# Top-k attention and capacity-limited MoE: the weights of a pair of units, all mask products first, then all second score products

## Chip, cores and metric

The kernel runs on one core of one Trainium2 chip. The metric is the device time of one execution in microseconds (us). Engines are named as in the profile: PE is the matrix engine, PEld its loads of stationary operands, DVE the vector engine, ACT the scalar engine, POOL the GpSimd engine.

## The reference, cut to what matters

```python
scores = (q @ k.T) / 8                      # 8 batches x 8 heads, 576 x 576, D = 64
kth    = 32nd largest of each row
scores = where(scores >= kth, scores, -1e9)
attn   = exp(scores - max); attn = attn / (sum + 1e-9)
x      = attn @ v                           # -> 4608 tokens x 512
...
# then a top-1 MoE: 8 experts, each keeps the 80 tokens of the highest gate weight,
# out[tok] = gate * (relu(x[tok] @ w1[e]) @ w2[e]), all other rows are 0
```

The change lies in the attention alone: in the step that turns a row's 32nd-largest score into the weights `exp(score)` of the scores that are kept.

## The kernel before

The attention treats two heads of a batch at a time, 32 such head pairs (`NP`) in all. A head pair has q, k and v of both heads side by side: `qT` and `kT` are 128 partitions by 576 columns, head 0 on partitions 0 to 63 and head 1 on 64 to 127. The 576 rows of a head are cut in four tiles of 128 and a tail of 64 (`t` = 0 to 4). A *unit* is one head's tile of 128 rows; the tails of both heads together are one unit. So a head pair has nine units, and a *pair of units* is the same tile of both heads.

For each unit:

- `front` (L190, L195): score products for the pair with rows on the partitions, into PSUM `sp` (one buffer), copied by ACT to `s`. These are the scores that are searched.
- `parts`, `search` (L202 to L227): DVE finds the 32nd-largest value, by maxima of six slices, three rounds of eight, and a last count that needs ACT (L218) and POOL (L219).
- `drop` (L249): DVE writes a bf16 `mask`, which is the row's maximum for scores that are kept and that plus one for scores that are dropped.

For each pair of units:

- `turn_w` (L265 to L273): the scores once more, now turned, with keys on the partitions, into PSUM `ab` (one buffer; a bank for each head, four chunks of 128 keys) and `cc` (the last 64 keys of both heads, two buffers, shared with the small logits tile `lp`). Two matmuls add up in each place. The mask product (L265) has the bf16 mask as stationary operand and a diagonal of large negative numbers (`minus`) as moving one, so it turns the mask and pushes dropped scores far below zero. The second score product (L269) has `kT` as stationary operand, in float32, 64 rows of the array for each head. ACT then takes the exponential (L272 for `ab`, L273 for `cc`) into `wT`.
- `back` (L287, L289): the weights times v, and their sum, into another part of `cc`.

`front` and `turn_w` both use matmuls over 64 rows of the array (one head each); the mask product uses all 128 rows; the products for the last 64 keys and those of `back` have 64 output columns.

The order is written out by hand. `run` goes through steps i = 0, 1, 2 ...; each engine gets its instructions in the order of the steps and works them off strictly in that order. In step i DVE starts unit i and advances the searches of units i-1, i-2 and i-3; PE gets, in this order, `turn_w` for the pair that unit i-3 completes, `front` for the pair that unit i+2 begins (or, where there is none, the turning of a next head pair's q and k), `back` for the pair that unit i-4 completes, and, once in a head pair, the turning of the normalised output `xn` and its logits `lp` (`norm`). Nine steps are one head pair; this is called a *round* below. The part that matters inside `turn_w`:

```python
for c in range(NK):                # 5 chunks of keys
    for h in range(2): mask product (h, c)     start=True
    for h in range(2): score product (h, c)    stop=True
```

After the attention `judge` and `finish` choose the tokens and do the experts. A second, slower attention (`batch`) stands in a branch for inputs where the search fails.

Of the kernel before, what the change touches and what calls it, by code (L numbers as in the profile page):

```python
# [24 lines left out]
def kernel(  # L25
# [11 lines left out]
    nc = tc.nc  # L37
    B, H, S, D = q.shape
# [8 lines left out]
    P = 128  # L47
    HP = H // 2
    NP = B * HP
    NF = S // P  # L50
    TL = S - NF * P
    NK = NF + 1
# [60 lines left out]
    class Attention:  # L113
# [137 lines left out]
        def turn_w(self, n, t):  # L251

            qT, kT = self.turned[n]
            i = n * UPP + 2 * t
            m = P if t < NF else TL
            masks = [self.mask.pop(i), self.mask.pop(i + 1)] if t < NF else [self.mask.pop(i)] * 2
            eye = [minus, minus] if t < NF else [minus[:, :TL], minus[:, TL:]]
            ab = self.ps_w.tile([P, 2, NF, P], F32, name="ab", tag="ab")
            cc = self.ps_c.tile([P, 512], F32, name="cc", tag="cc")
            rows = slice(t * P, t * P + m)  # L260
            for c in range(NK):
                ks = slice(c * P, min(c * P + P, S))
                for h in range(2):
                    d = slice(D * h, D * h + D)
                    nc.tensor.matmul(ab[:, h, c, :m] if c < NF else cc[d, :m], lhsT=masks[h][:, ks], rhs=eye[h],  # L265
                                     start=True, stop=False)
                for h in range(2):
                    d = slice(D * h, D * h + D)
                    nc.tensor.matmul(ab[:, h, c, :m] if c < NF else cc[d, :m], lhsT=kT[d, ks], rhs=qT[d, rows],  # L269
                                     start=False, stop=True)  # L270
            wT = self.rows.tile([P, 2 * NF + 1, P], F32, name="wT", tag="wT")
            nc.scalar.activation(wT[:, : 2 * NF, :m], ab.rearrange("p h c r -> p (h c) r")[:, :, :m], Act.Exp, scale=scale)  # L272
            nc.scalar.activation(wT[:, 2 * NF, :m], cc[:, :m], Act.Exp, scale=scale)  # L273
            self.w[n, t] = wT, cc
# [430 lines left out]
```

## Time and profile before

The time is 1617.32 us, the median of 3 runs (1616.72 to 1620.83). The profiled execution has a span of 1610.5 us at a mean granted clock of 0.826.

| What | Value |
|---|---|
| start and first loads | the first 23 us |
| attention | 23 to about 1432 us |
| choosing of tokens, experts | about 1432 to 1610 us |
| mask products, L265 | 1600 matmuls, the last at 1432.1 us |
| second score products, L269 | 3200 matmul records (two passes for each float32 product) |
| one exponential of `ab`, L272, at 128 rows | 1.02 us |
| one copy of scores to `s`, L195, of two full units | 1.13 us |

A float32 product appears as two matmul records, one for each pass. Matmuls overlap in the engine and their ends are modelled, so costs are read from the distance between starts. The granted clock is a share of full speed: 1.00 or 0.50 in any short stretch, and 0.83 on average over the attention.

### The profile page before, as it was taken

What the parts mean: (1) busy time and instruction counts of PE and PEld (TensorE: products, weight loads), DVE (VectorE), ACT (ScalarE), POOL (GpSimd) and SP (SyncE); (2) the same over time, 40 slices, a digit from 0 to 9 for tenths busy, and PEclk for the clock granted to TensorE, in tenths of its full rate; (3) what the DMA queues carried; (4) which work ended last, traced back from release to release, by engine and by line L of the source; (5) the groups of instructions that cost most, each with busy time, mean ns of one, the idle gap of its engine ahead of it and who ended that gap; (6) DMA issues with size and microseconds to landing.
All of it is one profiled execution on the core that took longest, in us unless ns stands there. A gap on an engine that the chain in (4) does not pass through costs nothing.

```text
span 1610.5 us, 38356 instructions
## 1 busy us (share of the span) xinstructions
PE 1311.5 (81%) x14862; PEld 936.5 (58%) x14862; DVE 1124.7 (70%) x5095; ACT 682.4 (42%) x1374; POOL 513.0 (32%) x501
## 2 busy tenths in 40 slices
PE   6889888888888888888888888888888888861787
PEld 4556555555555665555555556655555556550687
DVE  5777777777777777786777777777877777838211
ACT  3454444444444544444444445444444444420010
POOL 2333333333333333333333332333333333320111
PEclk9888788887888887888878888878888788775699
DMA  4022222222111122222221111111111110021270
GB/s 119 9 76 83 83 69 57 57 57 57 38 43 42 49 57 56 57 57 57 57 57 32 46 29 26 31 31 31 31 31 31 31 31 9 9 73 39 74 289 25
DMA packets 154591, 85.94 MB, mean 53 GB/s; under 512 B 118304, under 2 KB 136736, under 8 KB 154400
## 3 DMA queue, kind: packets, MB, share of 16 engines
q1 hardware_dynamic: 153376, 80.78, 17.6%
q0 software_dynamic: 1024, 2.62, 0.5%
q8 instruction: 118, 1.93, 0.5%
q14 instruction: 73, 0.60, 0.1%
HBM read 63.19 MB, written 20.19 MB: 52 GB/s over the span
## 4 chain that ended last, share of the span: by engine, by line
PE 70%; DVE 17%; ACT 11%; issue 2%; POOL 0%; DMA 0%; POOLq 0%; DVEq 0%; ACTq 0%
PE ab L269 19%; PE sp L190 15%; PE ab L265 9%; PE cc L287 9%; ACT s L195 5%; DVE mask L249 4%; DVE cand L202 4%; PE cc L269 4%; DVE pick L227 3%; PE sp L165 3%; PE lp L322 2%; PE yp L613 2%; ACT wT L272 2%; DVE cand L222 2%; PE cc L265 2%
## 5 line engine op out<-in xcount | busy, mean ns | idle before, releaser
L219 POOL TENSOR_TENSOR y<-s,y 128x576 f32<-128x576 f32 x288 | 416.7, 1447 | 891.9 <-ACT y L218 888.1
L202 DVE MAX8 cand<-s 128x8 f32<-128x96 f32 x1728 | 428.7, 248 | 253.2 <-ACT s L195 253.1
L269 PE MATMUL ab<-qT,kT 64*128 64x128 f32 (+1 forms) x2560 | 359.2, 363 | 0.0
L272 ACT ACTIVATE wT<-ab 128x1024 f32<-128x1024 f32 (+1 forms) x160 | 150.2, 939 | 415.8 <-PE ab L269 413.7
L265 PE MATMUL ab<-minus,mask 128*128 128x128 bf16 (+1 forms) x1280 | 197.8, 233 | 150.7 <-DVE mask L249 132.2
L190 PE MATMUL sp<-kT,qT 64*128 64x288 f32 (+1 forms) x1280 | 275.3, 565 | 48.3 <-ACT s L195 25.7
L224 DVE MAX8 w<-y 128x8 f32<-128x576 f32 x288 | 214.6, 745 | 92.9 <-POOL y L219 92.9
L269 PEld LDWEIGHTS ab<-qT,kT 64*128 64x128 f32 x2560 | 228.1, 218 | 68.5 <-issue 18.5
L249 DVE TENSOR_SCALAR mask<-s,thr,top 128x576 bf16<-128x576 f32 x288 | 264.9, 920 | 0.3
L265 PEld LDWEIGHTS <-mask 128*128 128x128 bf16 (+1 forms) x1600 | 103.8, 104 | 255.7 <-DVE mask L249 145.7
L287 PEld LDWEIGHTS cc<-vb,wT 128*64 128x64 f32 x4608 | 210.5, 163 | 67.2 <-issue 52.7
L195 ACT ACTIVATE s<-sp 128x1152 f32<-128x1152 f32 (+1 forms) x160 | 165.7, 1035 | 181.0 <-PE sp L190 180.8
L287 PE MATMUL cc<-vb,wT 128*64 128x65 f32 x4608 | 241.6, 251 | 0.0
L218 ACT ACTIVATE y<-s,w 128x576 f32<-128x576 f32 x288 | 222.8, 774 | 18.7 <-DVE w L213 18.6
L190 PEld LDWEIGHTS sp<-kT,qT 64*128 64x128 f32 (+1 forms) x1280 | 140.6, 233 | 128.9 <-ACT s L195 55.8
L227 DVE SCALAR_TENSOR_TENSOR pick<-past,cnt,w 128x9 f32<-128x9 f32 x288 | 140.4, 487 | 0.2
L222 DVE MATCH_REPLACE8 cand<-top,cand 128x48 f32<-128x48 f32 x576 | 110.2, 191 | 0.0
L213 DVE MAX8 top<-cand 128x8 f32<-128x48 f32 x576 | 110.0, 191 | 0.1
L287 PE MATMUL cc<-vr,wT 128*64 128x65 f32 x1152 | 101.8, 245 | 0.0
L269 PE MATMUL cc<-qT,kT 64*64 64x128 f32 (+1 forms) x640 | 79.7, 335 | 0.0
L289 ACT COPY xu<-cc 128x130 f32<-128x130 f32 (+1 forms) x160 | 42.3, 265 | 80.2 <-PE cc L287 80.1
L287 PEld LDWEIGHTS cc<-vr,wT 128*64 128x64 f32 x1152 | 74.8, 161 | 0.0
(165 smaller groups left out, 991.3 us busy)
## 6 DMA issues: line engine op xcount, KB each, us to landing
w<-in_moe_w_dram SPq DMA_DIRECT2D x32, 512.0 KB, 4.5
w<-in_moe_w_dram SPq DMA_DIRECT2D x8, 2048.0 KB, 11.9
out_dram<-zero SPq DMA_DIRECT2D x9, 1024.0 KB, 8.3
qn<-in_q_dram SPq DMA_DIRECT2D x64, 128.0 KB, 2.7
kn<-in_k_dram SPq DMA_DIRECT2D x64, 128.0 KB, 2.7
vb<-in_v_dram SPq DMA_DIRECT2D x64, 128.0 KB, 2.4
xd<-xn SPq DMA_DIRECT2D x32, 256.0 KB, 2.4
qn<-in_q_dram SPq DMA_DIRECT2D x32, 32.0 KB, 2.5
```

Source lines behind the costliest of these rows:

```text
L190: nc.tensor.matmul(o, lhsT=qT[d, t * P : t * P + m], rhs=kT[d, j * HS : (j + 1) * HS], start=True, stop=True)
L195: nc.scalar.activation(s[:, : g * S].rearrange("p (j c) -> p j c", c=HS), ps[:, : 2 * g, :HS], Act.Copy, scale=TINY)
L202: nc.vector.max(out=cand[:, j, :], in_=s[:, j * S // NG : (j + 1) * S // NG])
L218: nc.scalar.activation(y, s, Act.Sign, bias=w9[:, 7:8], scale=-1.0, accum_out=cnt)
L219: nc.gpsimd.tensor_tensor(out=y, in0=s, in1=y, op=Alu.mult)
L224: nc.vector.max(out=w9[:, 8:], in_=y)
L227: nc.vector.scalar_tensor_tensor(out=pick, in0=past, scalar=cnt, in1=w9[:, 7:], accum_out=self.thr[:, i : i + 1], op0=Alu.is_equal, op1=Al ...
L249: nc.vector.tensor_scalar(self.mask[i], s, self.thr[:, i : i + 1], top[:, 0, 0:1], op0=Alu.is_lt, op1=Alu.add)
L265: nc.tensor.matmul(ab[:, h, c, :m] if c < NF else cc[d, :m], lhsT=masks[h][:, ks], rhs=eye[h], start=True, stop=False)
L269: nc.tensor.matmul(ab[:, h, c, :m] if c < NF else cc[d, :m], lhsT=kT[d, ks], rhs=qT[d, rows], start=False, stop=True)
L272: nc.scalar.activation(wT[:, : 2 * NF, :m], ab.rearrange("p h c r -> p (h c) r")[:, :, :m], Act.Exp, scale=scale)
L287: nc.tensor.matmul(cc[r : r + TL, o], lhsT=wT[:, h * NF + c if c < NF else 2 * NF, r : r + TL], rhs=vb[:, c, h, :] if c < NF else vr[:, h, ...
```

## The change

In `turn_w` the loop over chunks that holds both kinds of product becomes two loops. The first does all mask products, head by head (for each head its five chunks); the second does all score products, chunk by chunk, the two heads in turn. The matmuls, their operands and their number are the same, and so is everything outside this loop. Since a bank of `ab` now has four open sums at once, `start=True` is kept only for the first product in each bank (chunk 0) and for the last chunk, which has its own bank. The purpose is that products of one kind follow each other in the array.

```diff
+            keys = [slice(c * P, min(c * P + P, S)) for c in range(NK)]
+            heads = [slice(D * h, D * h + D) for h in range(2)]
+            dst = [[ab[:, h, c, :m] for c in range(NF)] + [cc[heads[h], :m]] for h in range(2)]
+
+            for h in range(2):
+                for c in range(NK):
+                    nc.tensor.matmul(dst[h][c], lhsT=masks[h][:, keys[c]], rhs=eye[h], start=c in (0, NF), stop=False,
+                                     skip_group_check=True)
             for c in range(NK):
-                ks = slice(c * P, min(c * P + P, S))
                 for h in range(2):
-                    d = slice(D * h, D * h + D)
-                    nc.tensor.matmul(ab[:, h, c, :m] if c < NF else cc[d, :m], lhsT=masks[h][:, ks], rhs=eye[h],
-                                     start=True, stop=False)
-                for h in range(2):
-                    d = slice(D * h, D * h + D)
-                    nc.tensor.matmul(ab[:, h, c, :m] if c < NF else cc[d, :m], lhsT=kT[d, ks], rhs=qT[d, rows],
-                                     start=False, stop=True)
+                    nc.tensor.matmul(dst[h][c], lhsT=kT[heads[h], keys[c]], rhs=qT[heads[h], rows], start=False, stop=True,
+                                     skip_group_check=True)
```

## The prediction, made before the changed kernel was run

> **What bounds the kernel now.** I read the page first: busy times, then the chain that ended last (shares of the span by engine, then by line).
>
> ```profile
> PE 1311.5 (81%) x14862; PEld 936.5 (58%) x14862; DVE 1124.7 (70%) x5095; ACT 682.4 (42%) x1374; POOL 513.0 (32%) x501
> ...
> PE 70%; DVE 17%; ACT 11%; issue 2%; POOL 0%; DMA 0%; POOLq 0%; DVEq 0%; ACTq 0%
> PE ab L269 19%; PE sp L190 15%; PE ab L265 9%; PE cc L287 9%; ACT s L195 5%; DVE mask L249 4%; DVE cand L202 4%; PE cc L269 4%; DVE pick L227 3%; PE sp L165 3%; PE lp L322 2%; PE yp L613 2%; ACT wT L272 2%; DVE cand L222 2%; PE cc L265 2%
> ```
>
> PE carries 70% of the chain, and the lines of the change (L265, L269, into ab and cc) hold 34% of the span, some 548 us, or 3.4 us for each of the 160 calls of turn_w. So the change acts on the path. Next, the waits from 300 to 1400 us (total, times, longest):
>
> ```profile
> DVE cand L202 <- ACT s L195: 188.1, 71, 3.9
> PE ab L265 <- DVE mask L249: 95.9, 38, 3.9
> PE ab L265 <- ACT wT L272: 14.5, 25, 0.6
> ```
>
> PE waits for DVE's mask once in a round, DVE about three times for fresh scores: a loop. PE's timeline shows it (start, us, what, idle before):
>
> ```profile
> 647.37 1.24 PE L190 MATMUL sp<-kT,qT 64*128 64x288 f32 x8
> ...
> 649.86 0.23 PE L265 MATMUL ab<-minus,mask 128*128 128x128 bf16 x1
> 653.95 0.29 PE L265 MATMUL ab<-minus,mask 128*128 128x128 bf16 x1 [3.85 <-DVE mask L249]
> 654.16 0.80 PE L269 MATMUL ab<-qT,kT 64*128 64x128 f32 x4
> ```
>
> A front ends at 648.64, ACT copies it by 649.80, DVE needs 4.1 us for its step up to the mask (653.89), and only then turn_w goes on, with the next front behind it. One mask product (head 0) had run before the wait; head 1's held all the rest. Such waits end at 565.09, 609.04 and 653.95; over 28 rounds a round lasts 44.36 us.
>
> Last, the loads of stationary operands, around a chunk of turn_w and around the change from lp to masks:
>
> ```profile
> 620.48 0.11 PEld L265 LDWEIGHTS <-mask 128*128 128x128 bf16 x2
> 620.70 0.30 PEld L269 LDWEIGHTS ab<-qT,kT 64*128 64x128 f32 x4
> 621.12 0.11 PEld L265 LDWEIGHTS <-mask 128*128 128x128 bf16 x2
> ```
>
> ```profile
> 628.32 0.53 PEld L322 LDWEIGHTS lp<-wg,xT 128*128 128x128 f32 x4
> 628.68 0.21 PEld L265 LDWEIGHTS <-mask 128*128 128x128 bf16 x2
> 628.99 0.30 PEld L269 LDWEIGHTS ab<-qT,kT 64*128 64x128 f32 x4
> ```
>
> In the chunk PEld stands idle for 104 ns before the score loads and for 121 ns before the next mask loads. From lp to mask, both on all 128 rows and columns, the load starts (628.684) while the lp matmul that began at 628.682 runs. A change of the array's shape empties it; a change of type alone does not.
>
> **What the Trainium skill says.** TensorEngine Tiling (Array Packing), Key Properties: changing the tiling mode drains the engine. The trace agrees, with the two idle times above. TensorE: Matmul & The Clock Gate, Part 2, says that loads are pulled ahead of running matmuls; the lp case agrees. The same page, Part 1, has a free-running window of 3.41 us, after an idle one of which the clock is halved. The trace agrees on the window (below), though a stretch with 2.83 us of PE busy was also followed by half clock. PSUM — Partial Sum Buffer, The four PSUM rules: the start flag clears the marks of a whole bank, which is why the change keeps one start for each bank; this costs no time and no run here shows it.
>
> **The change, part by part.** Nothing is added or taken away; order and flags change. All starts are from the trace.
>
> A full-clock chunk before, 640 ns: the two masks start 66 ns apart (620.482, 620.548), 147 ns later the score loads start, and 422 ns later the next chunk's mask loads (two passes 213 ns apart, then the emptying). Four chunks 2.56 us, the last mask pair 0.175, the last score pair 0.365: 3.10 us.
>
> After, at full clock: four masks of a head need 66 + 55 + 55 ns (55 is the distance of the pair at 628.794, whose loads were ahead), then 147 to empty: 0.33 us. That head's fifth mask has 64 output columns, another shape: 0.18 us. For two heads 1.01 us. Scores: 422 ns for the first chunk and for three more chunks two passes each at about 107 (transposes of the same size, L165, start 109 apart): 1.06 us. Last pair 0.365. Sum 2.44 us, so 0.66 us less. Shape changes fall from nine to five.
>
> At half clock (chunks at 609.626 and 610.681: 1.06 us): before 4 x 1.06 + 0.25 + 0.48 = 4.97; after 2 x (0.54 + 0.25) + (0.73 + 6 x 0.213) + 0.48 = 4.07 us; 0.90 less. The pace of 107 was not seen for this product. Its ends are 107, and about 160 if each pass still waits for part of its load; then a block saves only 0.34 at full clock.
>
> A second gain: the order by head puts all of head 0's masks (0.50 us) before the first one of head 1. In the block that waits for head 1's mask they lie in the wait. Nothing is queued behind them that could have run.
>
> Now a round, in us from the end of the long wait (609.04 = 0), before and then after. Block t=1 runs 0 to 4.70, mostly at half clock; after, head 1's masks 0.5, scores 2.0, last pair 0.48: ends at 3.0. The tail front 4.70 to 6.65 follows, ACT has it at 7.33, DVE waits for it and makes the next mask at 10.28: all 1.7 earlier. Block t=2 starts 11.44, after 9.75, and ends 14.6, after 12.5. Then 5.3 us of xn, front, back and lp, unchanged. Block t=3 starts 19.9, after 17.8; its ab is done at 22.39, after 19.94 (2.14 into the block), and the exponential holds up the tail block until 23.49, after 21.04; DVE's mask for it, at 22.69 and after 20.99, is ready just in time. The tail block takes 3.47 us, partly at half clock; it has 64 moving columns, and I take 0.6 off, between 0.42 (full) and 0.93 (half). The front after it ends at 29.2, after 26.1. Back and turning of q and k are unchanged; block t=0 starts 35.3, after 32.2, and takes 2.44 for 3.10. Its front ends 39.6, after 35.85; scores at 40.8 and 37.0. DVE could begin that step at 39.2 before and 36.1 after, so the scores still end the wait. Plus 4.07 of DVE: 44.9 before, 41.1 after. The round loses 3.75 us of the 4.3 or so that PE saves. DVE's own work, 34.5 us busy and 2.5 of waits for POOL in a round, is no bound yet.
>
> **The clock.** Cut in windows of 3.41 us, the round shows (us, then busy of PE, PEld, DVE, ACT, POOL, then granted clock):
>
> ```profile
> 606.17:609.58 3.41, 0.54 (x5) 0.40 (x5) 3.41 (x7) 0.87 (x2) 3.26 (x3) 1.00 0.00 0
> 609.58:612.99 3.41, 3.41 (x23) 2.05 (x20) 3.32 (x19) 0.07 (x1) 0.66 (x2) 0.50 0.46 123
> ...
> 630.06:633.47 3.41, 2.83 (x32) 1.99 (x30) 3.41 (x13) 1.95 (x4) 1.35 (x1) 1.00 0.02 5
> 633.47:636.89 3.42, 3.42 (x26) 2.57 (x26) 3.07 (x10) 0.77 (x2) 1.40 (x1) 0.50 0.01 2
> ```
>
> The long wait brings half clock on, and so does the stretch around the wait for the exponential. 44.36 us is 13.0 windows: rounds seem tied to the windows. Twelve windows are 40.96, 3.41 less. Between 3.41 and 3.75 I take 3.6; 31 rounds (36 to 1406 us) give 111 us, and 1617 - 111 = 1506.
>
> **Rivals.**
>
> - *Favoured, 0.60*: as worked out, 1506.
> - *Smaller gain from grouping, 0.14*: passes at 160 ns, or drains that stay. Some 2.2 us a round: 1617 - 68 = 1549. For it: no run of such products without a shape change is in the trace. Against it: L165 at 109, and the front's loads, which run ahead.
> - *The clock gains too, 0.12*: the long wait falls from 3.85 to about 3.4 us and may no longer fill a window. Block t=1 then takes 1.9, its front 1.2: 1.8 us more a round, 5.4 x 31 = 167, so 1450. Against it: DVE's 37 us come close, and a full window idle wasn't needed for the other slowdown.
> - *The clock takes back most, 0.09*: the wait for the exponential grows from 0.58 to about 0.8 us, and another two windows a round fall to half clock: a block 1.63 and a front 1.0 more, 2.6 us. Gain 1.0 a round: 1586.
> - *Slower, 0.05*: two such stretches a round, 5.2 against 3.6: 31 x 1.6 = 50, so 1667. Only the sensitivity of the clock speaks for it.
>
> **How the numbers follow.** The prediction is the favoured case. The range goes from just under the third case to just under the fourth, 1445 to 1580; outside lie the slower case, most of the fourth and a margin of the third. Slower by over 0.3% is 0.05; within 0.3% is 0.03, from the upper edge of the fourth; faster 0.92.
>
> **What would show it.** Right: masks in fours about 55 ns apart; score passes 107 to 110 apart with no PEld idle between chunks; a full-clock block of 2.4 us; rounds of about 41 us; PE's wait for masks still once a round at about 3.4; DVE's waits for s smaller by 1.5 us or more a round. Wrong: passes at 160; a round of 43 or more with a lower granted clock than 0.83; new waits of PE for masks at blocks t=2 or the tail, which would mean that DVE has become the bound.

## The result, and the profile after

The changed kernel takes 1421.72 us, the median of 4 runs (1420.56 to 1422.79), against 1617.15 us before: a ratio of 0.879, with a 95% interval of 0.877 to 0.880. That is 195 us less, where 111 were predicted, and the time lies below the stated range of 1445 to 1580.

The first lines of the page of after are the busy times, then the clock granted in 40 slices, then the chain that ended last:

```profile
PE 1125.7 (79%) x14862; PEld 863.7 (61%) x14862; DVE 1130.2 (80%) x5095; ACT 678.0 (48%) x1374; POOL 506.5 (36%) x501
...
PEclk9999899989899998998998999889989989855899
...
PE 68%; DVE 14%; ACT 14%; issue 3%; POOL 1%; DMA 0%; POOLq 0%; DVEq 0%; ACTq 0%
PE sp L190 17%; PE ab L271 14%; PE cc L289 12%; PE ab L267 6%; ACT s L195 5%; DVE mask L249 4%; PE cc L267 3%; ACT wT L274 3%; PE cc L271 3%; PE lp L324 3%; PE yp L615 3%; DVE cand L202 3%; DVE pick L227 2%; ACT y L218 2%; PE sp L165 2%
```

The same matmuls keep PE busy for 186 us less. The lines of the change, now L267 and L271, fell from 34% of the span to 26%, and PE still leads the chain. The mean granted clock rose from 0.826 to 0.874, which the favoured case of the prediction had not counted on.

All of the gain is in the attention: from the last turned score product to the end it is 178.1 us before and 177.4 after. A round, over 24 rounds of the trace, fell from 44.38 to 38.67 us.

The waits of DVE and PE from 300 to 1200 us (total, times, longest):

```profile
DVE cand L202 <- ACT s L195: 90.3, 67, 2.3
PE ab L267 <- DVE mask L249: 80.8, 23, 3.5
PE ab L267 <- ACT wT L275: 20.3, 23, 0.9
```

They are the same three as before. DVE's waits for scores fell from 7.6 to 3.8 us a round. PE still waits once a round for a mask, 3.5 us instead of 3.9, and for the exponential 0.88 us instead of 0.58.

PE's timeline around the wait, then PEld's in an undisturbed block (start, us, what, idle before):

```profile
566.26 0.40 PE L267 MATMUL ab<-minus,mask 128*128 128x128 bf16 x4
566.59 0.24 PE L267 MATMUL cc<-minus,mask 128*64 128x128 bf16 x1
570.34 0.42 PE L267 MATMUL ab<-minus,mask 128*128 128x128 bf16 x4 [3.51 <-DVE mask L249]
```

```profile
578.09 0.94 PEld L267 LDWEIGHTS <-mask 128*128 128x128 bf16 x10
579.09 0.97 PEld L271 LDWEIGHTS ab<-qT,kT 64*128 64x128 f32 x16
580.18 0.20 PEld L271 LDWEIGHTS cc<-qT,kT 64*64 64x64 f32 x4
```

Head 0's five mask products now run ahead of the wait, as predicted. The sixteen loads of the score products go through in 0.97 us without a gap. By the single starts, masks follow each other at 66, 56 and 56 ns, score passes at 105 to 112 ns (the two heads side by side, 6 or 7 ns apart), and each change of shape among the masks costs 147 to 172 ns from the last start to the next load. From its first to its last matmul start a block at full clock takes 2.26 us, where it took 2.90 before (medians of blocks t=0).

What the prediction missed shows in windows of 3.41 us (us, then busy of PE, PEld, DVE, ACT, POOL, then granted clock), around the long wait and around the tail block:

```profile
567.18:570.59 3.41, 0.25 (x4) 0.23 (x4) 3.41 (x9) 0.87 (x2) 3.26 (x3) 1.00 0.00 0
570.59:574.00 3.41, 3.41 (x28) 2.72 (x27) 3.41 (x18) 0.93 (x2) 0.94 (x2) 0.50 0.36 99
574.00:577.42 3.42, 2.67 (x38) 1.58 (x36) 2.04 (x13) 2.20 (x6) 1.04 (x1) 1.00 0.72 164
587.66:591.07 3.41, 2.53 (x40) 1.92 (x36) 3.41 (x17) 1.94 (x4) 1.81 (x2) 1.00 0.00 0
591.07:594.49 3.42, 3.42 (x30) 2.27 (x30) 1.97 (x9) 1.60 (x3) 0.31 (x1) 0.50 0.00 0
594.49:597.90 3.41, 2.54 (x40) 1.93 (x37) 2.31 (x15) 1.83 (x6) 1.43 (x1) 1.00 0.00 0
```

Half clock still comes on at the same two places in a round, but it mostly ends after one window; in 8 of 24 rounds the first stretch still lasts three. Before, it lasted two or three windows at the first place and two at the second. Counted over 24 rounds, half clock fell from 15.1 to 9.1 us a round.

### The profile page after: what moved, and what is told of

The parts are those of the page before. It is cut to its first block, busy times and chain, and to the rows that moved or that the text cites. A ratio compares the mean times of both kernels' runs of the same rounds, so it can differ in the third digit from the quotient of the medians.

```text
span 1420.7 us, 38356 instructions
## 1 busy us (share of the span) xinstructions
PE 1125.7 (79%) x14862; PEld 863.7 (61%) x14862; DVE 1130.2 (80%) x5095; ACT 678.0 (48%) x1374; POOL 506.5 (36%) x501
## 4 chain that ended last, share of the span: by engine, by line
PE 68%; DVE 14%; ACT 14%; issue 3%; POOL 1%; DMA 0%; POOLq 0%; DVEq 0%; ACTq 0%
PE sp L190 17%; PE ab L271 14%; PE cc L289 12%; PE ab L267 6%; ACT s L195 5%; DVE mask L249 4%; PE cc L267 3%; ACT wT L274 3%; PE cc L271 3%; PE lp L324 3%; PE yp L615 3%; DVE cand L202 3%; DVE pick L227 2%; ACT y L218 2%; PE sp L165 2%
## 5 line engine op out<-in xcount | busy, mean ns | idle before, releaser
L219 POOL TENSOR_TENSOR y<-s,y 128x576 f32<-128x576 f32 x288 | 408.6, 1419 | 704.2 <-ACT y L218 702.4
L274 ACT ACTIVATE wT<-ab 128x1024 f32<-128x1024 f32 (+1 forms) x160 | 150.1, 938 | 297.8 <-PE ab L271 296.3
L190 PE MATMUL sp<-kT,qT 64*128 64x288 f32 (+1 forms) x1280 | 251.9, 523 | 48.4 <-ACT s L195 25.8
L267 PE MATMUL ab<-minus,mask 128*128 128x128 bf16 (+1 forms) x1280 | 124.8, 222 | 143.5 <-DVE mask L249 116.2
L289 PEld LDWEIGHTS cc<-vb,wT 128*64 128x64 f32 x4608 | 194.3, 152 | 65.3 <-issue 50.8
L218 ACT ACTIVATE y<-s,w 128x576 f32<-128x576 f32 x288 | 222.8, 774 | 20.1 <-DVE w L213 19.8
L267 PEld LDWEIGHTS <-mask 128*128 128x128 bf16 (+1 forms) x1600 | 109.0, 103 | 202.3 <-DVE mask L249 154.9
L249 DVE TENSOR_SCALAR mask<-s,thr,top 128x576 bf16<-128x576 f32 x288 | 231.7, 805 | 0.3
L289 PE MATMUL cc<-vb,wT 128*64 128x65 f32 x4608 | 222.7, 239 | 0.0
L271 PE MATMUL ab<-qT,kT 64*128 64x128 f32 (+1 forms) x2560 | 215.3, 315 | 0.0
L271 PEld LDWEIGHTS ab<-qT,kT 64*128 64x128 f32 x2560 | 182.5, 216 | 11.5
L227 DVE SCALAR_TENSOR_TENSOR pick<-past,cnt,w 128x9 f32<-128x9 f32 x288 | 185.4, 644 | 0.2
L267 PE MATMUL cc<-minus,mask 128*64 128x128 bf16 (+1 forms) x320 | 78.4, 245 | 0.0
L271 PE MATMUL cc<-qT,kT 64*64 64x128 f32 (+1 forms) x640 | 77.2, 325 | 0.0
```

The lines of the kernel that those rows point to most:

```text
L190: nc.tensor.matmul(o, lhsT=qT[d, t * P : t * P + m], rhs=kT[d, j * HS : (j + 1) * HS], start=True, stop=True)
L218: nc.scalar.activation(y, s, Act.Sign, bias=w9[:, 7:8], scale=-1.0, accum_out=cnt)
L219: nc.gpsimd.tensor_tensor(out=y, in0=s, in1=y, op=Alu.mult)
L227: nc.vector.scalar_tensor_tensor(out=pick, in0=past, scalar=cnt, in1=w9[:, 7:], accum_out=self.thr[:, i : i + 1], op0=Alu.is_equal, op1=Al ...
L249: nc.vector.tensor_scalar(self.mask[i], s, self.thr[:, i : i + 1], top[:, 0, 0:1], op0=Alu.is_lt, op1=Alu.add)
L267: nc.tensor.matmul(dst[h][c], lhsT=masks[h][:, keys[c]], rhs=eye[h], start=c in (0, NF), stop=False, skip_group_check=True)
```

## The experiments

Two theories stood for the shorter stretches. **Streaming**: half clock ends after a window in which PE streams enough columns; the old block, which emptied the array twice a chunk, streamed too few. **Round length**: a shorter round merely meets the windows elsewhere. In the diffs, `mask(h, c)` and `score(h, c)` stand for the two matmuls of `turn_w`, and `old()` and `new()` for the two orders of the change. The first four runs shared runs of the kernel before (1616.92 us), the next four others (1615.87), the last one others (1616.85).

### One block of the five in the new order, and the other four

```diff
-            new()
+            new() if t == 1 else old()      # only_t1
+            new() if t != 1 else old()      # but_t1
```

> New order in block t=1 alone (the one behind the long wait), old order in the other four. Theory 'streaming': half clock ends after a window in which PE streams enough columns; the old block at half clock streams too few because of its emptyings, the new one enough. It expects the first half-clock stretch of a round to shrink from 6.8 or 10.2 us to 3.4, the second to stay at 6.8, half clock per round 15 to about 11 us, and the time near 1546 us (1.45 us a round from the block itself and about 0.9 from the clock). Theory 'round length': the stretches shrank because a shorter round meets the windows of the clock elsewhere. It expects both stretches as before and 1617 - 31 x 1.45 = 1572 us.

> The complement: old order in block t=1, new order in the other four. 'Streaming' expects the first stretch to stay at 6.8 us or more and the second to shrink to 3.4, and, with 0.64 us from three blocks and 1.1 from the tail block, about 1617 - 31 x 3.0 = 1524 us or a little less. 'Round length' expects both stretches to shrink, since the round is nearly as short as with the whole change: 1450 to 1470 us.

Measured: 1516.55 us for the new order in block t=1 alone (ratio 0.938, 0.937 to 0.940), 1463.41 us for the complement (0.904, 0.902 to 0.907). In 24 rounds, the first stretch of half clock and the second lasted so many windows:

| Kernel | first stretch | second stretch | half clock, us a round |
|---|---|---|---|
| before | 2 (14 times), 3 (10) | 2 (24) | 15.1 |
| only_t1 | 1 (16), 2 (7), 3 (1) | 2 (15), none (9) | 9.0 |
| but_t1 | 2 (17), 3 (4), 4 (3) | 1 (13), none (11) | 10.1 |
| after | 1 (16), 3 (8) | 1 (24) | 9.1 |

The first stretch shortened where block t=1 was in the new order, and never fell under two windows where it was not. The second stretch of only_t1 kept its two windows in 15 rounds, with the old order at that place; in the other 9 it did not come at all, so where a block falls among the windows matters too. Round length alone doesn't explain the table: but_t1 has a round of 39.9 us, near that of after (38.7), and its first stretch stayed long. Here are the first two windows of a first stretch in only_t1, then in but_t1, and the second and third of the stretch of the kernel before whose first one, at 609.58, the prediction shows:

```profile
568.78:572.19 3.41, 3.31 (x27) 2.77 (x29) 3.41 (x20) 0.40 (x1) 1.29 (x2) 0.50 0.30 90
572.19:575.60 3.41, 2.65 (x30) 1.45 (x28) 2.10 (x13) 2.44 (x6) 0.76 (x1) 1.00 0.73 166
```

```profile
590.57:593.99 3.42, 3.42 (x22) 2.10 (x21) 3.42 (x19) 0.00 (x0) 0.85 (x2) 0.50 0.39 110
593.99:597.40 3.41, 3.02 (x18) 1.32 (x14) 0.09 (x1) 1.54 (x3) 0.00 (x0) 0.50 0.68 153
```

```profile
612.99:616.41 3.42, 2.67 (x14) 1.19 (x12) 0.02 (x1) 1.82 (x4) 0.00 (x0) 0.50 0.69 156
616.41:619.82 3.41, 3.41 (x30) 2.37 (x32) 3.41 (x16) 1.77 (x3) 1.40 (x1) 0.50 0.69 171
```

PE counts as busy throughout the first window of but_t1, with 22 matmuls, and half clock goes on; in only_t1 the new order has 27 in 3.31 us, and full clock follows. So PE's busy time, as the profile models it, doesn't show what the clock follows.

A count of moving columns does. Take each matmul's moving columns, times the share of the 128 rows that it uses, and twice for a float32 pass: such passes start 107 ns apart where bf16 products of 128 columns start 55 apart. Split a matmul at a window's edge by that pace, which is half as fast at half clock. In the kernel before, from 200 us on to 190 us before the end (357 windows), every window that half clock followed then has at most 3072, and every one that full clock followed at least 3174, whichever clock it ran at itself. In all eleven traces a limit of 3140 puts 3269 of 3287 windows right; the best limit on PE's busy time fails in 342, the best on the number of matmuls in 288. The window at 568.78 of only_t1 has 3242; that at 590.57 of but_t1 has 2532, and its second 3100 (one of the 18 that fail). In the kernel before, 609.58 has 2560, 612.99 has 2816 and 616.41 has 5003; the one at 630.06 of the prediction, busy for 2.83 us and followed by half clock, has 3072. The count was fitted to these traces, and no run here tests it on another kernel. It is what 'streaming' asks for: PE is busy throughout at 609.58 before and at 570.59 in after, both at half clock, and the old block moves 2560 columns in that time, the new one 3360.

'Streaming' had expected 1546 and 1524 us, 30 and 60 more than was measured. 'Round length' was 55 us too high for only_t1, but the 1463 of but_t1 lie in its 1450 to 1470. So the times don't decide between the two; the first stretches do. A part that neither had is in the table: in 9 and 11 of 24 rounds the second stretch does not come at all. The two gains, 100 and 153 us, sum to more than the 195 of the whole change, so they overlap.

### The order among the masks

```diff
-            for h in range(2):                 # the change: five changes of shape
-                for c in range(5): mask(h, c)
+            for h in range(2):                 # four_four: three
+                for c in range(4): mask(h, c)
+            for h in range(2): mask(h, 4)
+            for c in range(5):                 # by_chunk: three, heads in turn
+                for h in range(2): mask(h, c)
```

> New order, but the mask products as four of head 0, four of head 1, then both of the last 64 keys: three changes of shape within a block in place of five. If emptying sets the price of a change of shape, a full-clock block falls from 2.26 us (first to last start) to about 1.98; four such blocks a round give up to 1.1 us a round: 1388 to 1403 us. If DVE has become the bound, 1415 to 1425.

> New order, but the mask products chunk by chunk with the heads in turn: the same three changes of shape as four_four, but only one mask product can run ahead of the wait for head 1's mask. Blocks without the wait as in four_four. Block t=1 has about 0.2 us (full clock) to 0.4 (half clock) more behind the wait: 6 to 12 us slower than four_four. If running head 0's masks in the wait is worth nothing, the same as four_four.

Measured: 1390.58 us (0.860, 0.858 to 0.861) and 1393.99 us (0.862, 0.860 to 0.863). Two changes of shape fewer take a full-clock block from 2.26 to 1.985 us, as expected to the hundredth, and the kernel another 31 us below the change; in that, half clock fell as well, from 9.1 to 8.0 us a round. By the blocks, a change of shape among the mask products costs 0.14 us at full clock.

Running head 0's masks inside the wait is worth 3 us or nothing; the intervals touch. In by_chunk block t=1, where nearly all of it ran at half clock, does take up to 3.39 us, against 3.07 in four_four, but its rounds sit at 37.5 to 37.7 us, eleven windows, with each stretch one window long in all 24 rounds. In four_four eight of 24 first stretches last three windows, and half clock is 8.0 us a round against 6.8. So what by_chunk loses in the block it gets back from the clock.

### The last score products first, where the next front has the other shape

```diff
-            for c in range(5):
+            for c in ((4, 0, 1, 2, 3) if t in (0, 4) else range(5)):
                 for h in range(2): score(h, c)         # otherwise as four_four
```

> four_four, but in blocks t=0 and tail the score products of the last 64 keys come first, so that the block ends in the shape in which the next front begins. An emptying less, twice a round, 0.1 to 0.15 us each, against an exponential that starts some 0.36 us later behind the front: 1380 to 1391 us.

Measured: 1389.62 us (0.859, 0.857 to 0.862), against 1390.58 for four_four: no difference that can be told. A round takes 37.62 us, against 37.55 in four_four, so what an emptying less may have given was taken back; fifteen of 24 first stretches of half clock now last three windows, and half clock is 9.1 us a round against 8.0.

### Matmuls that nothing reads in PE's waits

These kernels keep all their work and add matmuls whose result lies in unused columns of `cc`, so that PE isn't idle while it waits.

```diff
+            if t == 4:
+                for _ in range(16): matmul(cc[:, 258:386], lhsT=minus, rhs=minus)
+            if t == 1:                          # 34 in before_fill, 30 in the others;
+                for _ in range(34):             # inside the masks in four_fill and edges_fill
+                    matmul(cc[:, 258:512], lhsT=minus, rhs=masks[0][:, :254])
```

before_fill, after_fill, four_fill and edges_fill have the order of before, after, four_four and edges. four_fill has the second filler alone, the others have both.

> The old order, with matmuls that nothing reads in the two waits: 34 of 254 columns (about 3.6 us) ahead of block t=1, 16 of 128 (about 0.9 us) ahead of the tail block. 'Streaming' expects both half-clock stretches to go: half clock per round from 15 us to near 0, and, with the block, front and tail at full clock, some 4 us a round: about 1493 us. That would be the clock's part of the old time. If the clock follows from something else than PE's idling, 1617 or, with fillers too long, more.

> four_four with 30 such matmuls of 254 columns in block t=1, between head 0's masks and head 1's. 'Streaming' expects the first stretch to go and the second to stay: half clock from 7.7 to about 3 us a round, 1 to 2 us a round off: 1330 to 1360 us. If DVE is the bound by now, 1380 to 1390.

> edges with both fillers (30 of 254 columns inside block t=1, 16 of 128 ahead of the tail block). 'Streaming' expects almost no half clock in a round and DVE (33.6 us busy and about 1 of waits) as the next bound: a round of 35 us, 1310 to 1330 us. If the clock isn't set by PE's idling, 1385 or more.

> The changed order with both fillers, 30 of 254 columns ahead of block t=1 and 16 of 128 ahead of the tail block, so that it stands beside before_fill with the clock nearly full in both. If the change is worth on its own account what the blocks show at full clock (0.64 us from each of three, some 0.5 from the tail block, 0.64 plus 0.5 from the one with the wait: 3.6 us a round), the round goes from 38.97 to about 35.4, near DVE's floor of some 34: about 1338 us, and the rest of the 195 us (1617 to 1422), some 80, is the clock's. If the clock's part is small, nearer 1260 to 1290; if the change mostly helps the clock, 1400 or more.

| Kernel | us | ratio to before | round, us | half clock, us a round |
|---|---|---|---|---|
| before | 1617 | 1 | 44.38 | 15.1 |
| before_fill | 1449.66 | 0.897 (0.894 to 0.899) | 38.96 | 0.85 |
| after | 1421.72 | 0.879 (0.877 to 0.880) | 38.67 | 9.1 |
| after_fill | 1306.35 | 0.808 (0.806 to 0.809) | 34.72 | 0 |
| four_fill | 1297.32 | 0.802 (0.801 to 0.804) | 34.42 | 0.28 |
| edges_fill | 1285.92 | 0.795 (0.794 to 0.797) | 34.12 | 0 |

The granted clock in 40 slices and the chain by engine and by line, of before_fill (L274 is the filler):

```profile
PEclk9999999999999999999999999999999999765799
...
PE 67%; DVE 20%; ACT 11%; issue 2%; POOL 1%; DMA 0%; POOLq 0%; DVEq 0%; ACTq 0%
PE ab L269 18%; PE sp L190 10%; PE ab L266 9%; PE cc L301 6%; ACT s L195 6%; DVE mask L249 5%; DVE cand L202 4%; DVE pick L227 4%; PE cc L269 4%; PE cc L274 3%; PE sp L165 3%; PE lp L336 3%; PE yp L627 3%; PE cc L266 2%; ACT y L218 2%
```

Clock and chain by engine of edges_fill:

```profile
PEclk9999999999999999999999999999999999755999
...
DVE 56%; PE 28%; ACT 12%; issue 2%; DMA 0%; POOL 0%; POOLq 0%; ACTq 0%; SPq 0%; DVEq 0%
```

With the waits filled, half clock is all but gone from the attention, and the old kernel alone loses 167 us. So half clock cost the kernel before at least about that much, and it costs the changed one at least 115 us (1421.72 to 1306.35): the fillers themselves hold 3% of the span on the chain of before_fill, some 43 us, and 2%, some 26 us, on that of after_fill. The order itself, with the clock nearly full in both, is worth 1449.66 - 1306.35 = 143 us; the other 52 of the 195 us are the clock's, 167 less 115. As the two fillers cost unlike amounts, by some 17 us, this split is no finer than that. All four came out 24 to 43 us under what 'streaming' expected, after_fill at 1306 for about 1338: at full clock the order is worth more than the 3.6 us a round that was put down for it. four_fill was expected at 1330 to 1360 and its second stretch to stay; in 22 of 24 rounds it did not come at all, though nothing filled that wait; why is not shown.

edges_fill is the fastest, 9.6% under the changed kernel. Its chain shows why it stops there: DVE leads with 56%. In its rounds of 34.12 us DVE is busy for 33.6, and it waits for scores 0.43.

## Why the prediction was wrong

**The direction and the mechanism were right.** The lines of the change lay on the path; emptying at a change of shape was what the old order paid; nothing new stands in the way. That a switch of the tiling mode drains the engine, as the Trainium skill states in TensorEngine Tiling (Array Packing), Key Properties, held here, and four_four put 0.14 us on it.

**The blocks' prices held.** 0.66 us less at full clock was predicted and 0.64 measured; the pace of 107 ns for a pass, not seen before for this product, came out at 105 to 112. So the second rival (passes at 160, 1549 us) falls. Block t=1 was given 3.0 us at half clock and takes 3.07. One sum slipped: block t=2, begun at 9.75 and 2.44 long, ends at 12.2 and not at 12.5. It hardly matters, since the mask at 20.99 would have held up the tail block until about the same time.

**The step that failed is the walk through the round, where it left the work after block t=1 at the clock that it had before.** Set the end of the long wait to 0 (570.34 us in after, 609.04 before), and take the start of the blocks:

| Start of block | before | predicted | measured |
|---|---|---|---|
| t=2 | 11.44 | 9.75 | 7.75 |
| t=3 | 19.8 | 17.8 | 15.42 |
| tail | 23.49 | 21.04 | 18.82 |
| t=0 | 35.2 | 32.2 | 28.74 |
| end of the next wait | 44.9 | 41.1 | 37.8 |

Here are the tail front and the front after block t=1, then the tail block's start and the front behind it, in the kernel before and in after (PE; start, us, what, idle before):

```profile
613.53 2.13 PE L190 MATMUL sp<-kT,qT 64*64 64x288 f32 x8
616.41 2.29 PE L190 MATMUL sp<-kT,qT 64*128 64x288 f32 x8 [0.75 <-ACT s L195]
632.53 0.22 PE L265 MATMUL ab<-minus,mask 128*128 128x64 bf16 x2 [0.58 <-ACT wT L272]
635.93 2.29 PE L190 MATMUL sp<-kT,qT 64*128 64x288 f32 x8
```

```profile
573.43 1.42 PE L190 MATMUL sp<-kT,qT 64*64 64x288 f32 x8
575.60 1.24 PE L190 MATMUL sp<-kT,qT 64*128 64x288 f32 x8 [0.75 <-ACT s L195]
589.16 0.29 PE L267 MATMUL ab<-minus,mask 128*128 128x64 bf16 x4 [0.88 <-ACT wT L275]
591.27 2.29 PE L190 MATMUL sp<-kT,qT 64*128 64x288 f32 x8
```

Two microseconds were gained unforeseen before block t=2: the tail front, the next front and the back were left at half clock (1.95, 2.3 and 1.8 us), but the stretch ended soon after block t=1 and they took 1.4, 1.2 and 1.3. Another 1.2 us came between the tail block and block t=0: I took 0.6 off a tail block partly at half clock, 3.47 us to 2.87; it ran at full clock, in 2.11 us, and only its front and the beginning of the back fell in that stretch. Its median from first to last start fell from 3.04 to 1.89 us. Two rounds in three are of this kind, 37.7 us; in the others, 40.5 us, the first stretch still takes three windows, which leaves 38.67 on average.

The sign of the term was right, its size was not: the clock's part was put at nothing. The windows in the prediction already showed that a stretch of 2.83 us busy was followed by half clock, so the clock could not be following the busy time; yet the walk had nothing else to go by and kept the old kernel's clock. The Trainium skill, TensorE: Matmul & The Clock Gate, Part 1, has full clock come back after one busy window. In the kernel before, the window at 609.58, with PE busy for all 3.41 us, was followed by another at half clock (612.99); the measurement decides.

The order's own worth was low too, at 3.6 us a round. At full clock it is 38.96 - 34.72 = 4.24 us, a figure that still holds the 0.85 us of half clock left in before_fill and what its longer filler costs. Pulling the sum from 3.75 down to 3.6 because twelve windows are 40.96 us was wrong: the rounds that came out are 37.7 and 40.5 us.

**The rivals.** "The clock gains too", 1450 us at 0.12, was nearest, but for a reason that doesn't hold: the long wait, at 3.51 us, still brings half clock on in every round. The stretches shortened instead, and in both places. "The clock takes back most" named the longer wait for the exponential, which did grow, to 0.88 us; its stretch shrank all the same. DVE as a bound was rightly left out for this change, and comes in at 34 us a round.

## What to carry to other kernels

Order matmuls so that those with the same rows and columns of the array follow each other, and count the changes of shape, at some 0.14 us each here at full clock. That it pays to end one stage in the shape of the next is not shown: edges gained nothing that can be told. When the granted clock alternates, don't price an edit at the clock that its neighbours had: denser work can end a slow stretch early, and that sped up fronts and backs that the edit never touched. Judge a window by the columns that move in it and not by PE's busy time. Before you reorder anything, try what matmuls that nothing reads do in PE's waits: here they alone gave 167 us, where the new order alone gave 195 and both together 311.

## What the hardware showed that was not expected

A window with PE busy for the whole 3.42 us (but_t1, 590.57) can be followed by another at half clock, and a stretch of half clock can last four windows (3 of 24 rounds there). One limit on the moving columns of a window, 3140 as counted above, tells the clock of the next window in 3269 of 3287 cases, at full clock and at half clock alike. A filler of 3.6 us in one wait and 0.9 us in the other takes half clock from 15.1 to 0.85 us a round. Rounds can settle on a whole number of windows: by_chunk stays at 37.5 to 37.7 us, eleven windows, in all rounds but the first and the last, and there a block that is 0.3 us longer than in four_four costs 3 us or nothing over the whole kernel.
